# Moving the chunk states' products behind the outputs' products, and splitting one product in two, in a fused SSD and PReLU kernel

## Chip, cores and metric

One core of a Trainium2 chip runs the whole kernel. The metric is device time in microseconds of one execution; the time before is the median of six runs, 374.7 us (374.41 to 375.7). Engines: TensorE (PE; its weight loads appear as PEld), VectorE (DVE), ScalarE (ACT), GpSimd (POOL), and SyncE (SP), whose queue issues nearly all DMAs.

## What is computed

First a Mamba-2 style scan (batch 4, 8 heads, 768 tokens, head size 32, state size 16), then an MLP with a leaky activation over its 3072 tokens:

```python
for c in range(nc):                                   # chunks in order
    cum = np.cumsum(log_a[:, :, sl], axis=-1)
    L = np.exp(cum[:, :, :, None] - cum[:, :, None, :]) * causal
    CB = np.einsum('bhin,bhjn->bhij', Cc, Bc)
    y_intra = np.einsum('bhij,bhjd->bhid', CB * L, xc)
    y_inter = np.einsum('bhin,bhnd->bhid', Cc, state) * np.exp(cum)[:, :, :, None]
    y[:, :, sl] = y_intra + y_inter
    Bx = np.einsum('bhjn,bhjd->bhjnd', Bc, xc) * decay_from_j[:, :, :, None, None]
    state = decay_full[:, :, None, None] * state + np.sum(Bx, axis=2)
# x: y as 3072 tokens of 256
h = x @ w_in                                          # 256 -> 2048
g = np.maximum(h, 0.0) + alpha * np.minimum(h, 0.0)
out = g @ w_out                                       # 2048 -> 256
```

All data are fp32, and each fp32 product shows as two passes ("x2") in the trace.

## The kernel before

**Work and stages.** The tokens fall into 24 chunks of 128, taken in 12 pairs; two pairs make a group of 512 tokens, and there are six groups. Pair p yields the scan's outputs of its tokens, group g puts them through the MLP. In group 0 the MLP is done plainly, mixed with the conversion of the weights and with pairs 0 to 3. In groups 1 to 5 both MLP products are done as 2x2 block products with seven multiplications in place of eight (a Winograd form). While group g goes through the MLP, the two pairs of group g + 1 are computed in between.

**A quad.** A group's MLP has four quads z = 0 to 3, each for four blocks of 128 of the hidden size (`quad`, L758). A quad makes seven hidden products, each of two matmuls of 128x256 (L770), in two PSUM banks A and Y: b11 into A, t1 into Y, t2 onto A, t3 onto A, b22 onto Y, then t4 onto A. Y is emptied in between (g12 is made of it by `prelu`: ScalarE L753, then VectorE L755), and ScalarE writes m1 back into it (L799) so that b21 can be added onto it. After b21 comes the last `prelu`, which makes g11 of Y. The differences of g11, g12, g21, g22 are made on GpSimd (L804, L813). They are the inputs of the seven products with `w_out` (`product`, L734), which run one quad later.

**The order is written out by hand.** Each engine works its queue in the order of the program. `quad` calls `after(j)` at fourteen slots j, and `after` (L1024) puts everything else there: `places` says in which slot which of the seven products of the quad in front goes, `steps` in which slot a pair takes its next stage, `ahead` in which the GpSimd product `bn` (B times decays, L385) of a coming pair is made. b21 stands between slots 10 and 11.

**A pair's stages** (`pair`, L416; a generator, `ssm` takes steps of it). Pairs 4 to 11 are called fine. A fine pair has nine stages before the change:

1. transposes of B and C (L469), a copy (L472)
2. to 5. four quarters of the decay scans on VectorE (`half_decays`, L438), with the last ScalarE's `spread_c`
6. `states(added(...))`: `added` (L514) makes the state products (L519), column tiles of 128x64, in a PSUM tile of its own; `states` (L524) reads them on VectorE (ScalarE where the batch starts), and masks the result on GpSimd (`sm`). Then GpSimd's `c_decayed` (`cd`)
7. `products_bc` (L562): the Gram products (L569), row tiles of 32x128, four of them side by side, r = 0 to 3: r = 0 and 1 in small banks ("ss"), r = 2 and 3 in the hidden banks ("hp", those that A and Y have); and VectorE's first two multiplications by them (L604)
8. the other two multiplications
9. the outputs y: products with the state (L620, tiles of 64x128) and with the decayed Gram (L627, 128x32) in two ss banks, and two ScalarE copies into `xts` (L634)

The last pair of each batch (5, 8, 11) needs the state products of one chunk, not two: eight passes at L519 become four.

For the pair `nxt` = 2g + 2, stages 3 to 5 stand in slots 1, 2, 5 of quad 0, stage 6 in slot 9, stage 7 in slot 13, stages 8 and 9 in slots 1 and 5 of quad 1. The pair after it has stages 1 and 2 in slots 12 and 14 of quad 1 and the rest in quads 2 and 3 likewise. Quads 0 and 2 are called even here, 1 and 3 odd. In even quads with a pair (`with_gram`) product 7 stands in slot 11, behind b21; elsewhere (`without`) in slot 9, ahead of it. The first quad of group 1 has no products of a quad in front; rest of group 0's outputs (L684) take their places (`last_out`).

**PSUM.** ss and hp tiles rotate over two banks each; `bank(i)` are four fixed banks for the seven products' sums (and for group 0's outputs, which `store_first`, L688, copies out).

Of the kernel before, what the change touches and what calls it, by code (L numbers as in the profile page):

```python
# [9 lines left out]
F32 = mybir.dt.float32  # L10
# [12 lines left out]
def kernel(  # L23
# [25 lines left out]
    nc = tc.nc  # L49
# [276 lines left out]
    held = {}  # L326
    bns = {}

    def identity_bank():


        m5_bank.append(bank(3))
        nc.scalar.copy(out=m5_bank[0][:, HT:], in_=ident_h[:, :HT])
        ident_p.append(m5_bank[0][:, HT:])
# [77 lines left out]
    def spare():  # L412

        return ps_h.tile([P, GT], F32, name="hp", tag="hp")

    def pair(gp):  # L416

        b, c = divmod(2 * gp, CPB)
        nat, abc, xt, ap = loads["p", gp]
        last = c + 2 == CPB  # L420
        dec = work.tile([P, 2, H, Q], F32, name="dec")
        dv = dec.rearrange("p k h t -> p k (h t)")

# [37 lines left out]
            yield  # L461


        tp = spare() if gp == 1 else ss_tile()
        if gp == 0:
            keep_warm(tp, 3, Q)
# [19 lines left out]
        def c_decayed():  # L486
            nc.gpsimd.tensor_tensor(out=cd.rearrange("p k t -> p (k t)"), in0=ct, in1=pf,
                                    op=ALU.mult)

        fine = gp >= 2 * GC // 2  # L490
        if gp < 2:
            spread_c()
        if gp == 0:
# [1 line left out]
            dps = spare()  # L495
            keep_warm(dps, 6, Q)
            yield
        bn = bns.pop(gp) if gp in bns else pair_loads(gp)
        if gp == 1:
            c_decayed()  # L500
            dps = spare()
# [1 line left out]
        elif gp:  # L503
            yield

        nk = 1 if last else 2
        st = [masked.get(b)]  # L510
        new = work.tile([P, 2, P], F32, name="state")
        sm = work.tile([P, 2, P], F32, name="sm")

        def added(dps):  # L514
            dps = dps.rearrange("p (k m) -> p k m", m=P)
            for k in range(nk):
                for w in range(KC):
                    ws = slice(64 * w, 64 * w + 64)
                    nc.tensor.matmul(dps[ws, k], bn[:, k, ws], xt[:, k, w * P : (w + 1) * P],  # L519
                                     start=True, stop=True, tile_position=(0, 64 * w),  # L520
                                     skip_group_check=True)
            return dps

        def states(dps):  # L524
            for k in range(nk):
                old = state.get(b)
                if old is None:
                    nc.scalar.copy(out=new[:, k], in_=dps[:, k])
                else:
                    e = (k + 1) * Q - 1  # L530
                    nc.vector.scalar_tensor_tensor(out=new[:, k], in0=old, scalar=pf[:, e : e + 1],
                                                   in1=dps[:, k], op0=ALU.mult, op1=ALU.add)
                state[b] = new[:, k]
            nc.gpsimd.tensor_tensor(out=sm[:, :nk], in0=new[:, :nk],
                                    in1=hmask.unsqueeze(1).to_broadcast([P, nk, P]), op=ALU.mult)
            st.extend(sm[:, k] for k in range(nk))
            masked[b] = st[-1]

        if fine:
            for k in range(2):  # L540
                for w in range(2):
                    half_decays(k, w)
                    if k == 1 and w == 1:
                        spread_c()
                    yield
        else:
            if gp > 1:
                states(added(ss_tile()))
                c_decayed()
            decays(0)  # L550
            if gp == 1:
                dps = added(dps)
            if gp:
                yield
            if gp != 1:
                decays(1)
            if gp > 1:
                spread_c()
# [24 lines left out]
        if gp == 0:  # L583
            gram = products_bc()
            dps = added(dps)
            yield
            c_decayed()
            times(dec[:, :, :2], one_less(gram))
        elif gp == 1:
            decays(1)  # L590
            gram = products_bc()
            g0 = one_less(gram)
            states(dps)
            times(dec[:, :, :2], g0)
        else:
            if fine:
                states(added(ss_tile()))
                c_decayed()
            yield
            gram = products_bc()  # L600
        for i, r in enumerate(r for r in ((2, 3, 0, 1) if fine else (3, 2, 1, 0) if gp > 1 else range(4))
                              if r in gram):
# [6 lines left out]
        yield  # L609


        y = [ss_tile()[:, : 2 * Q].rearrange("p (k t) -> p k t", k=2) for w in range(KC)]
        if gp < 2:
            keep_warm(y[0].rearrange("p k t -> p (k t)"), 2 - gp)
        begun = False
# [7 lines left out]
        for k in range(2):  # L623
            for w in range(KC):
                for q in range(4):
                    h = 4 * w + q
                    nc.tensor.matmul(y[w][32 * q : 32 * q + 32, k], xt[:, k, h * D : (h + 1) * D],  # L627
                                     dec[:, k, h], start=False, stop=True,
                                     tile_position=(0, 32 * q), skip_group_check=True)
        g, q = divmod(2 * gp, GC)  # L630
        if q == 0:
            xts[g] = xtp.tile([P, KC, GT], F32, name="xT")
# [98 lines left out]
    LAST = {**HALVES, 4: (3, 1)}  # L731
    blocks = {}

    def product(g, z, n):  # L734

        if z == 0 and n == 1:
            ms[g] = [t.rearrange("p (h t) -> p h t", h=2)
                     for t in [bank(i) for i in range(3)] + m5_bank]
        i, h = (LAST if g == NG - 1 else HALVES)[n]
        s1, s2, s4 = out_sums  # L740
        for p in range(2):
            q = 2 * z + p
            w = {1: wq[:, q, 0, 0], 2: wq[:, q, 1, 0], 3: s4[:, q], 4: wq[:, q, 1, 1],
                 5: s1[:, q], 6: s2[:, q], 7: wq[:, q, 0, 1]}[n]
            nc.tensor.matmul(ms[g][i][:, h], w, blocks[g, z][n][:, p],  # L745
                             start=(q == 0 and h == 0), stop=(q == NQ - 1),
                             skip_group_check=True)
# [227 lines left out]
    for f in range(FIRST, NF):  # L975
        if f in (5, 10):
            load_pair(3 + f // 10)
        if f == 5:
            load_rows(1)
        hidden(0, f)  # L980
        if f <= 10:
            ssm(2)
        if f >= 9:
            ssm(3)
        if f < FIRST + 2:
            convert_a(*pieces[f + 1 + (f > FIRST)])
        convert_next(first=f > FIRST)
        if f == FIRST:
            convert_a(*pieces[6])
        if f == 8:  # L990
            bns[3] = pair_loads(3)
        if f == 8:
            rows_clamp(1)
            held["pr"] = rows_scan(1)
            rows_out(1)
        output(f - FIRST)
        if f in in_steps:
            weight_sums(wi, in_sums, 0, in_steps[f])
    early[0] = None
    token_sums(1)  # L1000
    ssm(2 * GC // 2, 2)


    steps = {(0, 1): 0, (0, 2): 0, (0, 5): 0, (0, 9): 0, (0, 13): 0, (1, 1): 0, (1, 5): 0,
             (1, 12): 1, (1, 14): 1, (2, 1): 1, (2, 2): 1, (2, 5): 1, (2, 9): 1, (2, 13): 1,
             (3, 1): 1, (3, 5): 1, (3, 12): 2, (3, 14): 2}

    late_sums = {(0, 2): ((wqt, out_sums, 0, 0),), (0, 4): ((wqt, out_sums, 0, 1),),
# [6 lines left out]
    last_out = {3: ((0, 0),), 5: ((1, 0),), 7: ((2, 0),), 8: ((3, 0),), 11: ((0, 1),), 13: ((1, 1),),  # L1015
            14: ((2, 1), (3, 1))}

    with_gram = {3: 1, 5: 2, 7: 3, 8: 5, 11: 7, 13: 6, 14: 4}
    without = {3: 1, 5: 2, 7: 3, 8: 5, 9: 7, 13: 6, 14: 4}
    for i in range(NZ * (NG - 1)):  # L1020
        g, z = divmod(NZ + i, NZ)
        nxt = 2 * g + 2

        def after(j, g=g, z=z, i=i, nxt=nxt):  # L1024
            places = with_gram if nxt < NP and z % 2 == 0 else without
            if i and j in places:
                product(*divmod(NZ + i - 1, NZ), places[j])
            if i == 0:
                for f, half in last_out.get(j, ()):
                    output(NF - LATE + f, half)  # L1030
            if (i, j) in ((0, 13), (1, 8)):
                store_first(i)
            for args in late_sums.get((i, j), ()):
                weight_sums(*args)
            if g > 1 and z == 0 and j in (5, 9, 13, 14):
                if j == 5:
                    comb[0] = combine(g - 1)
                next(comb[0], None)
            if g > 1 and z in (1, 3) and j == 11:
                finish(g - 1, z // 2)  # L1040
            if nxt + steps.get((z, j), NP) < NP:
                ssm(nxt + steps[z, j])
            if nxt < NP and (z, j) == (3, 7):
                token_sums(g + 1)
            ahead = nxt + {(1, 3): 1, (3, 8): 2}.get((z, j), NP)
            if ahead < NP:
                if ahead == 6:
                    rows_turn(1, held["pr"])
                bns[ahead] = pair_loads(ahead)

        comb = [None] if i == 0 else comb
        if z == 0 and nxt < NP:
            load_pair(nxt + 1)
        if z == 2 and nxt + 2 < NP:
            load_pair(nxt + 2)
        quad(g, z, after)
# [31 lines left out]
```

## Time and profile before

| | |
|---|---|
| median of six runs | 374.7 us (374.41 to 375.7) |
| the profiled execution | 374.95 us; span from first to last instruction 373.2 us; granted TensorE clock 1.000 |
| PE idle in waits that the profile lists | under 5 us, the largest 1.7 us for bn at L519 and 1.2 us for the first operand |
| 560 passes of the seven products (L745) | 82.5 us (with `w_out`) and 58.3 us (with its sums) busy |
| 64 passes of the state products in ss banks (L519) | 5.7 us busy |
| DMA | 30.71 MB in all, HBM read 26.98 MB |

A line of the timeline has start (us from the span's start), duration, engine, line, operation, tiles written and read, shape and count, and in brackets the engine's idle time ahead of it with what ended it. Several instructions of one kind in a row are one line. Matmuls are pipelined, so that durations of PE overlap: the time that a run costs is the difference of two starts.

### The profile page before, as it was taken

To read this page: it belongs to the slowest core of one execution; us is meant where nothing else is said; L and a number is where in the kernel's file an instruction comes from. 1 tells how busy PE (TensorE), PEld (TensorE's weight loads), DVE (VectorE), ACT (ScalarE), POOL (GpSimd) and SP (SyncE) were. 2 spreads that over 40 slices of the span, in tenths; PEclk is the share of its full clock that TensorE was granted. 3 is DMA by queue.
4 is the path that set the end of the run, shared out by engine and by line. 5 is a ranking of instruction groups with operands and counts; after the bars stand their busy time and mean duration, and the time that the engine had idled before them with its cause. 6 is when DMAs were issued, how large, how long until landed. Compare 5 with 4: busy or idle time off the path is not lost.

```text
span 373.2 us, 6183 instructions
## 1 busy us (share of the span) xinstructions
PE 365.1 (98%) x2223; PEld 294.1 (79%) x2223; DVE 243.3 (65%) x462; ACT 179.3 (48%) x384; POOL 200.9 (54%) x211
## 2 busy tenths in 40 slices
PE   8899999999999999999999999999999999999996
PEld 7676666578778788788788788788788788888884
DVE  7897889976438647838638847637847644543364
ACT  1557856435255345444445445445535525553541
POOL 4875566777928744724645535455355355264512
PEclk9999999999999999999999999999999999999999
DMA  7989998911019501003703702801911001001003
GB/s 139 195 173 338 240 302 163 173 47 58 28 48 186 105 3 56 2 0 58 154 3 57 155 2 51 163 0 30 157 28 29 2 0 22 10 0 30 1 0 84
DMA packets 121878, 30.71 MB, mean 82 GB/s; under 512 B 93736, under 2 KB 117752, under 8 KB 121848
## 3 DMA queue, kind: packets, MB, share of 16 engines
q1 hardware_dynamic: 116736, 29.74, 36.6%
q10 hardware_dynamic: 5112, 0.59, 1.1%
q8 instruction: 17, 0.28, 0.3%
q14 instruction: 13, 0.11, 0.1%
HBM read 26.98 MB, written 3.34 MB: 81 GB/s over the span
## 4 chain that ended last, share of the span: by engine, by line
PE 87%; DMA 3%; DVE 3%; POOL 2%; ACT 1%; ACTq 1%; issue 1%; POOLq 0%; DVEq 0%
PE hp L770 33%; PE bank L745 32%; PE bank L684 6%; PE hp L646 4%; PE ss L627 2%; DMA raw<-in_moe_w_in_dram 2%; PE ss L569 2%; PE ss L620 1%; DVE dec L438 1%; PE ss L519 1%; PE hp L569 1%; PE hp L661 1%; PE ss L469 1%; DMA nat<-in_C_dram 1%; ACTq L163 1%
## 5 line engine op out<-in xcount | busy, mean ns | idle before, releaser
L813 POOL TENSOR_TENSOR gt<-gt 128x512 f32<-128x512 f32 x58 | 73.6, 1269 | 31.4 <-DVE gt L755 24.5
L755 DVE SCALAR_TENSOR_TENSOR gt<-hp,s_mul,gt 128x256 f32<-128x256 f32 x120 | 52.5, 479 | 47.6 <-ACT gt L753 46.3
L745 PE MATMUL bank<-gt,w_out 128*128 128x256 f32 x320 | 82.5, 382 | 0.4 <-ACT o_sb L691 0.4
L753 ACT ACTIVATE gt<-hp,s_alpha 128x256 f32<-128x256 f32 x120 | 50.3, 470 | 46.8 <-PE hp L770 32.7
L745 PEld LDWEIGHTS bank<-gt,w_out 128*128 128x128 f32 x320 | 60.0, 190 | 11.2 <-issue 2.3
L804 POOL TENSOR_TENSOR gt<-gt 128x512 f32<-128x512 f32 x20 | 25.4, 1271 | 79.1 <-DVE gt L755 79.1
L745 PE MATMUL bank<-gt,ws 128*128 128x256 f32 x240 | 58.3, 379 | 0.0
L745 PEld LDWEIGHTS bank<-gt,ws 128*128 128x128 f32 x240 | 45.1, 190 | 5.8
L438 DVE TENSOR_TENSOR_SCAN dec<-abc,bank 128x256 f32<-128x256 f32 x80 | 48.1, 661 | 0.0
L770 PE MATMUL hp<-xs,w_in 128*128 128x256 f32 x160 | 42.9, 390 | 0.0
L770 PE MATMUL hp<-xT,w_in 128*128 128x256 f32 x160 | 41.9, 384 | 0.0
L770 PE MATMUL hp<-xs,ws 128*128 128x256 f32 x160 | 41.1, 379 | 0.0
L789 DVE TENSOR_TENSOR hp<-hp,u 128x512 f32<-128x512 f32 x20 | 14.0, 699 | 39.8 <-ACT u L787 39.8
L778 ACT COPY m<-hp 128x512 f32<-128x512 f32 x20 | 11.7, 586 | 51.8 <-PE hp L770 51.8
L770 PEld LDWEIGHTS hp<-xs,w_in 128*128 128x128 f32 x160 | 28.7, 189 | 7.7 <-issue 3.0
L770 PEld LDWEIGHTS hp<-xT,w_in 128*128 128x128 f32 x160 | 29.7, 190 | 5.1 <-issue 1.2
L770 PEld LDWEIGHTS hp<-xs,ws 128*128 128x128 f32 x160 | 30.4, 190 | 4.1
L684 PE MATMUL bank<-w_out,gt 128*128 128x256 f32 x128 | 31.0, 384 | 0.0
L684 PEld LDWEIGHTS bank<-w_out,gt 128*128 128x128 f32 x128 | 23.7, 190 | 6.6 <-issue 3.5
L793 DVE TENSOR_TENSOR c<-hp,m 128x512 f32<-128x512 f32 x20 | 13.6, 682 | 19.3 <-PE hp L770 19.3
L646 PE MATMUL hp<-xT,w_in 128*128 128x512 f32 x48 | 22.8, 597 | 0.8 <-DVE gt L650 0.6
L787 ACT COPY u<-hp 128x512 f32<-128x512 f32 x20 | 11.7, 585 | 23.0 <-PE hp L770 23.0
(156 smaller groups left out, 552.9 us busy)
## 6 DMA issues: line engine op xcount, KB each, us to landing
abc<-z SPq DMA_DIRECT2D x20, 512.0 KB, 5.2
raw<-in_moe_w_in_dram SPq DMA_DIRECT2D x8, 512.0 KB, 5.3
raw<-in_moe_w_out_dram SPq DMA_DIRECT2D x8, 512.0 KB, 6.8
xt<-in_x_dram SPq DMA_DIRECT2D x24, 128.0 KB, 2.9
out_dram<-o_sb SPq DMA_DIRECT2D x32, 64.0 KB, 1.9
nat<-in_B_dram SPq DMA_DIRECT2D x22, 64.0 KB, 2.7
nat<-in_C_dram SPq DMA_DIRECT2D x22, 64.0 KB, 2.8
ap<-pf SPq DMA_DIRECT2D x11, 128.0 KB
```

Source lines behind the costliest of these rows:

```text
L438: nc.vector.tensor_tensor_scan(out=dv[:, k, hs], data0=abc[k][:, hs], data1=ident_p[0], initial=0.0, op0=ALU.mult, op1=ALU.add)
L646: nc.tensor.matmul(hp, w_in[:, k, f * P : (f + 1) * P], xts[g][:, k], start=(k == 0), stop=(k == KC - 1))
L684: nc.tensor.matmul(pos[0][t // 2][:, t % 2], gt[:, t * Q : (t + 1) * Q], w_out[:, f], start=(f == 0 and t % 2 == 0), stop=(f == NF - 1), s ...
L745: nc.tensor.matmul(ms[g][i][:, h], w, blocks[g, z][n][:, p], start=(q == 0 and h == 0), stop=(q == NQ - 1), skip_group_check=True)
L753: nc.scalar.mul(o[:, p], h[:, p], s_alpha[:, fs[p]])
L755: nc.vector.scalar_tensor_tensor(out=o[:, p], in0=h[:, p], scalar=s_mul[:, fs[p]], in1=o[:, p], op0=ALU.mult, op1=ALU.max)
L770: nc.tensor.matmul(to[:, p], w(2 * z + p), b, start=start and p == 0, stop=True, skip_group_check=True)
L778: nc.scalar.copy(out=m1, in_=A)
L789: nc.vector.tensor_tensor(out=Y, in0=Y, in1=u2, op=ALU.add)
L793: nc.vector.tensor_tensor(out=c22, in0=A, in1=m5, op=ALU.add)
L804: nc.gpsimd.tensor_tensor(out=tc_, in0=g22, in1=g12, op=ALU.subtract)
L813: eng.tensor_tensor(out=o, in0=x0, in1=x1, op=ALU.subtract)
```

## The change

- A fine pair takes eleven stages. `added` and `states` come first and in stages of their own, before the transposes; `c_decayed` moves to the last quarter of the decay scans; y's products and their copies become two stages.
- In slot 5 of the odd quads four stages follow each other: y's products of the pair in front, the state products of the next pair, the copies of y, the states of the next pair. The state products are written into the free second half of y's second PSUM tile (`beside`), so they need no tile of their own. Pair 4, which has no fine pair in front, takes its first four stages ahead of the first quad.
- Slot 9 of the even quads loses its stage. In even quads with a pair one half of product 7 goes into slot 9 (ahead of b21), the other stays in slot 11.
- `bn` of the coming pair is made in slot 9 of the even quads rather than in slots 3 and 8 of quads 1 and 3 (pair 4's during block 14 of group 0).
- `store_first(1)` moves from slot 8 to slot 2 of the second quad of group 1.

```diff
         if fine:
+            bn = bns.pop(gp) if gp in bns else pair_loads(gp)
+            dps = added(beside.pop(gp) if gp in beside else ss_tile()[:, : 2 * Q])
+            yield
+            states(dps)
+            yield
...
         if fine:
             for k in range(2):
                 for w in range(2):
                     half_decays(k, w)
                     if k == 1 and w == 1:
                         spread_c()
+                        c_decayed()
                     yield
...
         else:
-            if fine:
-                states(added(ss_tile()))
-                c_decayed()
-            yield
+            if not fine:
+                yield
             gram = products_bc()
...
-        y = [ss_tile()[:, : 2 * Q].rearrange("p (k t) -> p k t", k=2) for w in range(KC)]
+        ys = [ss_tile() for w in range(KC)]
+        y = [t[:, : 2 * Q].rearrange("p (k t) -> p k t", k=2) for t in ys]
+        if fine:
+            beside[gp + 1] = ys[1][:, 2 * Q :]
...
+        if fine:
+            yield
         g, q = divmod(2 * gp, GC)
...
-    def product(g, z, n):
+    def product(g, z, n, parts=(0, 1)):
...
-        for p in range(2):
+        for p in parts:
...
+        if f == 14:
+            bns[4] = pair_loads(4)
...
-    ssm(2 * GC // 2, 2)
+    ssm(2 * GC // 2, 4)
-    steps = {(0, 1): 0, (0, 2): 0, (0, 5): 0, (0, 9): 0, (0, 13): 0, (1, 1): 0, (1, 5): 0,
-             (1, 12): 1, (1, 14): 1, (2, 1): 1, (2, 2): 1, (2, 5): 1, (2, 9): 1, (2, 13): 1,
+    steps = {(0, 1): 0, (0, 2): 0, (0, 5): 0, (0, 13): 0, (1, 1): 0, (1, 5): 0,
+             (1, 12): 1, (1, 14): 1, (2, 1): 1, (2, 2): 1, (2, 5): 1, (2, 13): 1,
              (3, 1): 1, (3, 5): 1, (3, 12): 2, (3, 14): 2}
...
-    with_gram = {3: 1, 5: 2, 7: 3, 8: 5, 11: 7, 13: 6, 14: 4}
-    without = {3: 1, 5: 2, 7: 3, 8: 5, 9: 7, 13: 6, 14: 4}
+    both = (0, 1)
+    without = {j: (n, both) for j, n in {3: 1, 5: 2, 7: 3, 8: 5, 9: 7, 13: 6, 14: 4}.items()}
+    with_gram = {**without, 9: (7, (0,)), 11: (7, (1,))}
...
-            if (i, j) in ((0, 13), (1, 8)):
+            if (i, j) in ((0, 13), (1, 2)):
                 store_first(i)
...
                 ssm(nxt + steps[z, j])
+                if j == 5 and z % 2:
+                    for p in (1, 0, 1):
+                        if nxt + z // 2 + p < NP:
+                            ssm(nxt + z // 2 + p)
...
-            ahead = nxt + {(1, 3): 1, (3, 8): 2}.get((z, j), NP)
+            ahead = nxt + {(0, 9): 1, (2, 9): 2}.get((z, j), NP)
```

More of the change, by code (lines that the diff above doesn't have):

```diff
@@ L327 @@
     bns = {}
+    beside = {}
     def identity_bank():
@@ L420, in pair @@
         last = c + 2 == CPB
+        fine = gp >= 2 * GC // 2
         dec = work.tile([P, 2, H, Q], F32, name="dec")
@@ L461, in pair, with added, states @@
             yield
+        nk = 1 if last else 2
+        st = [masked.get(b)]
+        new = work.tile([P, 2, P], F32, name="state")
+        sm = work.tile([P, 2, P], F32, name="sm")
+        def added(dps):
+            dps = dps[:, : 2 * Q].rearrange("p (k m) -> p k m", m=P)
+            for k in range(nk):
+                for w in range(KC):
+                    ws = slice(64 * w, 64 * w + 64)
+                    nc.tensor.matmul(dps[ws, k], bn[:, k, ws], xt[:, k, w * P : (w + 1) * P],
+                                     start=True, stop=True, tile_position=(0, 64 * w),
+                                     skip_group_check=True)
+            return dps
+        def states(dps):
+            for k in range(nk):
+                old = state.get(b)
+                if old is None:
+                    nc.scalar.copy(out=new[:, k], in_=dps[:, k])
+                else:
+                    e = (k + 1) * Q - 1
+                    nc.vector.scalar_tensor_tensor(out=new[:, k], in0=old, scalar=pf[:, e : e + 1],
+                                                   in1=dps[:, k], op0=ALU.mult, op1=ALU.add)
+                state[b] = new[:, k]
+            nc.gpsimd.tensor_tensor(out=sm[:, :nk], in0=new[:, :nk],
+                                    in1=hmask.unsqueeze(1).to_broadcast([P, nk, P]), op=ALU.mult)
+            st.extend(sm[:, k] for k in range(nk))
+            masked[b] = st[-1]
+        if fine:
[4 more added lines that the diff above has]
+            yield
         tp = spare() if gp == 1 else ss_tile()
@@ L488, in c_decayed @@
                                     op=ALU.mult)
-        fine = gp >= 2 * GC // 2
         if gp < 2:
@@ L497, in pair @@
             yield
-        bn = bns.pop(gp) if gp in bns else pair_loads(gp)
+        if not fine:
+            bn = bns.pop(gp) if gp in bns else pair_loads(gp)
         if gp == 1:
@@ L504, in pair @@
             yield
[L509 to L537, printed above, removed]
         if fine:
@@ L595, in pair @@
         else:
-            if fine:
-                states(added(ss_tile()))
-                c_decayed()
-            yield
+            if not fine:
+                yield
             gram = products_bc()
@@ L629, in pair @@
                                      tile_position=(0, 32 * q), skip_group_check=True)
+        if fine:
+            yield
         g, q = divmod(2 * gp, GC)
@@ L1026, in after @@
             if i and j in places:
-                product(*divmod(NZ + i - 1, NZ), places[j])
+                product(*divmod(NZ + i - 1, NZ), *places[j])
             if i == 0:
```

## The prediction

> **What bounds the kernel now.** I read the busy shares and the chain of waits first, then TensorE's timeline around the places that the change touches.
>
> ```profile
> PE 365.1 (98%) x2223; PEld 294.1 (79%) x2223; DVE 243.3 (65%) x462; ACT 179.3 (48%) x384; POOL 200.9 (54%) x211
> ...
> PE 87%; DMA 3%; DVE 3%; POOL 2%; ACT 1%; ACTq 1%; issue 1%; POOLq 0%; DVEq 0%
> ```
>
> TensorE (PE) sets the end: from 82 us on it starts a pass of a 128x256 product every 0.216 us (four passes, one product of two steps, take 0.86 us from start to start). The number of products doesn't change. So only what lies between them counts: changes of the array's tiling, and waits. The wait list of PE holds under 5 us in all, but a wait inside a run of small products isn't in it. The timeline of an even quad (pair 6) shows the part that is rearranged; the columns are start, duration (the last end is modelled, so I use differences of starts), engine, line.
>
> ```profile
> 149.71 1.03 PE L770 MATMUL hp<-xs,w_in 128*128 128x256 f32 x4
> 150.67 0.66 PE L519 MATMUL ss<-xt,bn 128*64 128x128 f32 x8
> 151.25 1.13 PE L770 MATMUL hp<-xT,w_in 128*128 128x256 f32 x4
> 152.22 1.03 PE L745 MATMUL bank<-gt,w_out 128*128 128x256 f32 x4
> 153.09 1.03 PE L745 MATMUL bank<-gt,ws 128*128 128x256 f32 x4
> 154.04 0.48 PE L569 MATMUL ss<-cz,bc 32*128 32x256 f32 x2
> ...
> 155.34 1.13 PE L745 MATMUL bank<-gt,w_out 128*128 128x256 f32 x4
> ```
>
> In order: the t4 product, the state products, the b21 product, product 7, product 6, the Gram products, product 4. Zooming into the Gram run, its fourth row tile (r = 3, in a hidden-product bank "hp") starts late, and the engines beside it tell why:
>
> ```profile
> 154.29 0.48 PE L569 MATMUL hp<-cz,bc 32*128 32x256 f32 x1
> ```
> ```profile
> 152.48 0.84 ACT L753 ACTIVATE gt<-hp,s_alpha 128x256 f32<-128x256 f32 x2 [0.38 <-PE hp L770]
> ```
> ```profile
> 153.35 0.88 DVE L755 SCALAR_TENSOR_TENSOR gt<-hp,s_mul,gt 128x256 f32<-128x256 f32 x2 [0.45 <-ACT gt L753]
> ```
> ```profile
> 95.04 0.18 PEld L569 LDWEIGHTS hp<-cz,bc 32*128 32x128 f32 x1 [0.26 <-DVE gt L755]
> ```
>
> That bank is Y, which b21 has just filled. It is free only when ScalarE and VectorE have made g11 of it: 153.35 + 0.88 = 154.23, and r = 3 starts 0.06 later. Tile 0 stood ready at 154.04, so 0.24 us is lost. In the first quad of group 1 the same wait (last line) is 0.55 us, as other VectorE work stands ahead. This release sits a fixed 154.29 - 151.25 = 3.04 us behind b21's start; nothing else is in its way, since both engines idle for it (0.38 and 0.45 us).
>
> **What the Trainium skill says.** The Trainium skill, page "TensorEngine Tiling (Array Packing)", Tiling Modes, Key Properties: a change of tiling mode, not of tile alone, drains TensorE. The trace agrees: the state products come 0.10 us after t4's last slot, and the first b21 pass takes 0.32 instead of 0.216 us. The Trainium skill, "TensorE: Matmul & The Clock Gate", Step-by-step: what each phase is for: MATMULs stay in program order. At 95.04 to 95.06 the chunk's second half of the Gram products starts only once r = 3 has, so one late tile holds all behind it. The Trainium skill, "PSUM — Partial Sum Buffer", PSUM bank collisions raise a hardware error: two engines may not touch one bank and quadrant at once, even in other columns. No run here shows it; it matters because the state products now share a bank with y.
>
> **The change, part by part.**
>
> 1. State products leave slot 9 of the even quads (pairs 5 to 11; pair 4 apart). From t4's start to product 4's start such a quad now takes 155.34 - 149.71 = 5.63 us with eight passes (pairs 6, 7, 9, 10), 5.41 with four (120.93 to 126.34; the last pair of a batch: 5, 11), 5.50 for pair 8, whose VectorE instruction was late. New course from t4: 0.86, half of product 7 0.43, so b21 starts at 1.30. It needs the copy of m1 into Y (L799), which ends at 0.90 to 1.00 (1.36 in pair 8's quad): no wait. Then b21 0.86, other half 0.43, product 6 0.86, entry 0.09: the Gram products arrive at 3.55. r = 3 needs b21's start + 3.04 less the 0.10 of the drain that is gone: 1.30 + 2.93 = 4.23. The wait grows from 0.24 to 0.68. From r = 3 to product 4 takes 155.34 - 154.29 = 1.05: product 4 at 5.28. Gain: 0.35 for pairs 6, 7, 9, 10; 0.13 for 5 and 11; 0.22 for 8. So half the price of the removed products comes back as a longer wait.
>
> 2. They are added behind the y products (L620, L627) of the pair in front:
>
> ```profile
> 160.72 0.49 PE L620 MATMUL ss<-cd,sm 64*128 64x128 f32 x4
> 161.14 1.08 PE L627 MATMUL ss<-dec,xt 128*32 128x128 f32 x32
> 162.15 1.13 PE L770 MATMUL hp<-xs,w_in 128*128 128x256 f32 x4
> 163.12 0.38 PE L770 MATMUL hp<-xT,ws 128*128 128x256 f32 x1
> ```
>
> The run leaves the full array and comes back anyway (0.97 instead of 0.86 for L770). Added: four steps of 0.109 us (two column tiles side by side; two steps for the last pair of a batch) and one inner change of mode. No row shows 128x32 to 128x64; the nearest, L620 to L627, costs 0.09, and I take 0.11. It can't gain, as the passes are extra; at most it is the price alone in slot 9, 0.34. So 0.55 and 0.33 us (up to 0.78 and 0.56). Net of 1 and 2: 4 x 0.20 + 2 x 0.20 + 0.11 = 1.3 us slower.
>
> 3. Copies and state steps: ScalarE's two copies (0.65 us) may wait for the 0.2 to 0.5 us of state products, and VectorE's two steps (0.34 to 0.72) go ahead of c22. Even one behind the other they end about 1.6 us after the products, and c22 0.7 later; ScalarE wants c22 only after g12, 3.1 us after. Hidden by t3 and b22; without that cover, up to 0.7 us in seven quads. GpSimd's sm, cd and bn steps (0.72, 0.72, 0.64) move into slots where it idles 5 us, or behind L804; nat of pairs 8 to 11 has landed by then (pair 9's last issue at 205.2, some 2.7 us to land, wanted after 208.8). Zero.
>
> 4. Pair 4: its state products now go ahead of the first quad, isolated as before: +0.78 at 81.72. GpSimd makes bn at about 80.4, 0.64 long, so at about 81.0: no wait (bound: 0.5 if the weight sums go first). token_sums is 0.64 later; its first result, at 82.95, is wanted after 83.8. In slot 9 nothing stands between t4 and b21: b21 starts at 1.05 instead of 1.54: L799's end at 0.90 plus 0.15, which t3 takes to start behind u2's copy in pair 6's quad (146.04 to 146.18). The weight sum on VectorE (0.69) then sets g11; r = 3 at 4.43 instead of 4.89: gain 0.47. Net +0.31.
>
> 5. store_first(1) moves from slot 8 to slot 2 of the second quad:
>
> ```profile
> 107.55 1.03 PE L770 MATMUL hp<-xs,w_in 128*128 128x256 f32 x4
> 109.02 1.13 PE L745 MATMUL bank<-gt,w_out 128*128 128x256 f32 x4 [0.44 <-ACT o_sb L691]
> 109.99 1.03 PE L770 MATMUL hp<-xT,w_in 128*128 128x256 f32 x4
> ```
>
> 107.55 to 109.99 is 2.44 where two products are 1.73: gain 0.71. The copy (0.58) fits into ScalarE's 1.20 us of idling ahead of u2. The DMA queue is held by this store until 108.99 and gets free sooner for pair 6's loads; nobody waits for those. rows_turn (about 0.12 us of PE) only changes place.
>
> Sum: 1.3 + 0.31 - 0.71 = +0.9 us. The profiled execution took 374.95 (span 373.2 and 1.75 around it), so 375.85; that run lies 0.25 above the median of 374.7, so the median becomes **375.6**.
>
> **Rivals.**
> - **The Gram wait doesn't grow (faster).** Y's release keeps its distance to the Gram products: product 4 at 3.55 + 0.24 + 1.05 = 4.84, a gain of 0.79 or 0.57 against 0.55 or 0.33 added, so -0.24 in seven quads; with 4 and 5, -2.1: 372.6. This is what the split of product 7 would give if only b21's own wait counted. Deciding point: r = 3 freed 0.13 us earlier than I say balances the change. Against: the chain PE, ACT, DVE has no slack in any of the quads looked at. 15%.
> - **The y block pays full price (slower).** The switch to 128x64 costs as an isolated one: 0.23 more in seven quads, 377.2. For: the mode does change. Against: L620 to L627. 12%.
> - **Hardly a change.** The inner switch is free (-0.1 x 7), the early insertion half hidden: 374.8. 18%.
> - My case, 375.6, with 375.1 to 376.2 as its own bounds: 55%. That the change doesn't do what it says can't be: the order of TensorE's queue is written out.
>
> **How the numbers follow.** About 0.2% (0.75 us) is what a measurement of this kernel can tell from no change, and my case straddles that line: seven tenths of it lie above 375.45. Slower: 0.55 x 0.7 + 0.12 = 0.50. Faster: 0.15 and a little of the third rival, 0.19. Same: 0.31. The range leaves out the faster rival and half of the dear one: 374.2 to 377.0.
>
> **What would show it.** Right: in even quads b21 starts 1.30 after t4, and r = 3 of the Gram products about 0.7 us after the other three tiles; y and state products together take 0.55 or 0.33 more than y did; no wait for o_sb. Wrong: r = 3 less than 0.5 late, or the run behind y over 0.7 longer, or a wait of b21 for L799, or late c22 in odd quads.

## The result, and the profile after

The changed kernel takes 375.94 us (median of 15 runs, 375.59 to 377.22); the kernel before, in the same session, 374.52 us (34 runs). The ratio is 1.0035, 95% interval 1.0025 to 1.0046: slower, by about 1.3 us. Forecast were 375.6 us and +0.9. The profiled execution took 376.65 us with a span of 374.7 (before: 374.95 and 373.2).

```profile
PE 367.1 (98%) x2223; PEld 295.5 (79%) x2223; DVE 247.1 (66%) x462; ACT 180.3 (48%) x384; POOL 201.2 (54%) x211
...
PE 89%; DVE 4%; DMA 2%; POOL 2%; ACT 1%; issue 1%; POOLq 0%; DVEq 0%; ACTq 0%
```

The page says little: the same 2223 passes on a TensorE that looks just as busy. The timeline of the same even quad (pair 6; lines have moved, L519 is now L478, L745 L758, L770 L783, L569 L579) shows what happened. Columns as before: start, duration, engine, line.

```profile
150.45 1.03 PE L783 MATMUL hp<-xs,w_in 128*128 128x256 f32 x4
151.31 0.59 PE L758 MATMUL bank<-gt,w_out 128*128 128x256 f32 x2
151.74 1.03 PE L783 MATMUL hp<-xT,w_in 128*128 128x256 f32 x4
152.61 0.59 PE L758 MATMUL bank<-gt,w_out 128*128 128x256 f32 x2
153.04 1.03 PE L758 MATMUL bank<-gt,ws 128*128 128x256 f32 x4
153.99 0.48 PE L579 MATMUL ss<-cz,bc 32*128 32x256 f32 x2
...
155.73 1.13 PE L758 MATMUL bank<-gt,w_out 128*128 128x256 f32 x4
```

t4, half of product 7, b21, the other half, product 6, Gram products, product 4. From t4 to product 4 it is now 155.73 - 150.45 = 5.28 us, where it was 5.63. The eight passes that left cost 0.78 us by themselves; the other 0.43 went into the wait of r = 3, the fourth row tile of the Gram products. Here are its first pass and the VectorE instruction that frees its bank:

```profile
154.67 0.48 PE L579 MATMUL hp<-cz,bc 32*128 32x256 f32 x1
154.68 0.48 PE L579 MATMUL ss<-cz,bc 32*128 32x256 f32 x2
```
```profile
153.74 0.88 DVE L768 SCALAR_TENSOR_TENSOR gt<-hp,s_mul,gt 128x256 f32<-128x256 f32 x2 [0.35 <-ACT gt L766]
```

g11 is done at 154.62, r = 3 starts at 154.67, 0.66 us behind its turn (before: 0.24); the other tiles' second half stands in the queue behind it (154.68). The odd quad holds the products that moved:

```profile
161.10 0.49 PE L631 MATMUL ss<-cd,sm 64*128 64x128 f32 x4
161.53 1.08 PE L638 MATMUL ss<-dec,xt 128*32 128x128 f32 x32
162.54 0.66 PE L478 MATMUL ss<-xt,bn 128*64 128x128 f32 x8
163.12 1.13 PE L783 MATMUL hp<-xs,w_in 128*128 128x256 f32 x4
```

162.54 to 163.12 is what is new: 0.59 us, unrounded. So a pair with two chunks' states wins 0.35 us in the even quad and pays 0.59 in the odd one.

**Where the time went.** The last run of group 0's outputs starts at times that differ by up to 1.6 us from one execution to the next (79.1 to 80.7 us in thirteen of the fourteen traces of this study, 79.7 and 80.1 in the two of the changed kernel itself; the fourteenth, with the state products issued twice, comes to 81.8), so spans of single executions can't be compared. The stretches from there on are the same to 0.01 us in the two traces of the changed kernel, and where other kernels have the same quad, to 0.04. From b11 to b11 of successive quads, after less before:

| stretch | forecast | measured |
|---|---|---|
| ahead of the first quad: pair 4's states | +0.78 | +0.74 |
| first quad | -0.47 | -0.27 |
| second quad: y with pair 5's states; store_first(1) | +0.33 - 0.71 | +0.37 - 0.71 |
| even quads of pairs 6, 7, 9, 10 | 4 x -0.35 | 4 x -0.35 |
| even quads of pairs 5, 8, 11 | -0.13, -0.22, -0.13 | -0.02, -0.22, -0.14 |
| odd quads, two chunks' states (four) | 4 x +0.55 | 4 x +0.59 |
| odd quads, one chunk's (8, 11) | 2 x +0.33 | 2 x +0.37 |
| rows_turn out of an odd quad | (counted even) | -0.12 |
| sum | +0.9 | +1.3 |

`rows_turn` is one small transpose (L370, 96x96) that goes with `bn` of pair 6, and so moved from an odd quad into pair 5's even quad. It had cost about 0.12 us where it was: -0.02 and -0.12 together are the -0.13 forecast. In its new place it stands ahead of b21 (122.50, b21 at 122.59). The sum of the stretches is the measured difference.

### The profile page after: what moved, and what is told of

The parts are those of the page before. It is cut to its first block, busy times and chain, and to the rows that moved or that the text cites. A ratio compares the mean times of both kernels' runs of the same rounds, so it can differ in the third digit from the quotient of the medians.

```text
span 374.7 us, 6170 instructions
## 1 busy us (share of the span) xinstructions
PE 367.1 (98%) x2223; PEld 295.5 (79%) x2223; DVE 247.1 (66%) x462; ACT 180.3 (48%) x384; POOL 201.2 (54%) x211
## 4 chain that ended last, share of the span: by engine, by line
PE 89%; DVE 4%; DMA 2%; POOL 2%; ACT 1%; issue 1%; POOLq 0%; DVEq 0%; ACTq 0%
PE hp L783 33%; PE bank L758 32%; PE bank L697 5%; PE hp L659 4%; PE ss L638 2%; DMA raw<-in_moe_w_in_dram 2%; PE hp L579 2%; PE ss L631 1%; PE ss L579 1%; DVE dec L441 1%; PE ss L478 1%; PE hp L674 1%; PE ss L511 1%; PE hp L270 1%; DVE gt L663 1%
## 5 line engine op out<-in xcount | busy, mean ns | idle before, releaser
L758 PE MATMUL bank<-gt,w_out 128*128 128x256 f32 x320 | 83.5, 381 | 0.0
L758 PEld LDWEIGHTS bank<-gt,w_out 128*128 128x128 f32 x320 | 60.1, 190 | 10.4 <-issue 2.3
L758 PE MATMUL bank<-gt,ws 128*128 128x256 f32 x240 | 58.3, 379 | 0.0
L758 PEld LDWEIGHTS bank<-gt,ws 128*128 128x128 f32 x240 | 45.1, 190 | 5.8
L783 PE MATMUL hp<-xs,w_in 128*128 128x256 f32 x160 | 42.8, 390 | 0.0
L783 PE MATMUL hp<-xT,w_in 128*128 128x256 f32 x160 | 41.2, 380 | 0.0
L783 PE MATMUL hp<-xs,ws 128*128 128x256 f32 x160 | 41.1, 379 | 0.0
L783 PEld LDWEIGHTS hp<-xs,w_in 128*128 128x128 f32 x160 | 28.7, 189 | 7.5 <-issue 2.3
L783 PEld LDWEIGHTS hp<-xs,ws 128*128 128x128 f32 x160 | 30.4, 190 | 4.1
L783 PEld LDWEIGHTS hp<-xT,w_in 128*128 128x128 f32 x160 | 30.2, 190 | 4.4 <-ACT hp L812 0.3
L493 POOL TENSOR_TENSOR sm<-state,bmask 128x256 f32<-128x256 f32 (+1 forms) x12 | 7.6, 637 | 35.0 <-DVE state L490 35.0
```

Source lines behind the costliest of these rows:

```text
L758: nc.tensor.matmul(ms[g][i][:, h], w, blocks[g, z][n][:, p], start=(q == 0 and h == 0), stop=(q == NQ - 1), skip_group_check=True)
L783: nc.tensor.matmul(to[:, p], w(2 * z + p), b, start=start and p == 0, stop=True, skip_group_check=True)
```

## Experiments

Each kernel was timed beside runs of the kernel before, whose medians were 374.53 to 374.85 us. The theory, called chain theory below: product 4 of an even quad comes at b21's start + 2.93 (b21, ScalarE, VectorE, then r = 3) + 1.05 us, as long as r = 3 has to wait. Passes ahead of b21 then count in full, and passes between b21 and the Gram products are free until the wait is filled. The main rival: TensorE's own sum of passes and mode changes, with order of no account.

**Product 7 whole behind b21.**

```diff
-    with_gram = {**without, 9: (7, (0,)), 11: (7, (1,))}
+    with_gram = {j: p for j, p in without.items() if j != 9}
+    with_gram[11] = (7, both)
```

> The changed kernel with product 7 whole in slot 11, behind b21, and nothing in slot 9. Chain theory (product 4 of an even quad stands a fixed 2.93 + 1.05 us behind b21's start, whatever lies between): b21 waits for the copy of m1 and starts at about 1.06 after t4 in place of 1.30, product 4 comes at 5.1 to 5.2 in place of 5.28, so 0.7 to 1.2 us less over seven quads: about 375.0. Rival, TensorE's own sum (order doesn't matter, the loss is only the state products' price in the y block): b21's new wait of 0.2 to 0.3 us is lost and nothing comes back, 1.5 to 2 us more: 377.5.

Measured: 374.7 us, ratio to before 1.0002 (0.9992 to 1.0012): 1.2 less than the changed kernel. Pair 6's quad:

```profile
149.02 1.03 PE L783 MATMUL hp<-xs,w_in 128*128 128x256 f32 x4
150.09 1.13 PE L783 MATMUL hp<-xT,w_in 128*128 128x256 f32 x4
151.05 1.03 PE L758 MATMUL bank<-gt,w_out 128*128 128x256 f32 x4
...
153.12 0.48 PE L579 MATMUL hp<-cz,bc 32*128 32x256 f32 x1
...
154.18 0.48 PE L758 MATMUL bank<-gt,w_out 128*128 128x256 f32 x1
```

b21 does wait (0.20 us after t4's last slot), and its first pass then takes 0.32 us instead of 0.216, as after a change of tiling; so r = 3 (153.12) comes 3.03 us behind its start and not 2.93. Yet product 4 comes at 5.16 in place of 5.28, and the seven even quads together are 1.28 us shorter than in the changed kernel: against the kernel before nothing is left of the loss (0.03 us by the stretches). A TensorE that idles and starts b21 sooner is faster here than one that does useful passes first.

**Product 7 whole ahead of b21** (`with_gram = without`).

> The changed kernel with product 7 whole in slot 9, ahead of b21. Chain theory: b21 starts 0.43 us later (1.73 after t4), and product 4 with it (5.71), though TensorE does the same work: 7 x 0.43 = 3.0 us more, 378.9, and r = 3 of the Gram products waits 1.1 us. Rival, TensorE's own sum: no difference, 375.9.

Measured: 379.09 us, ratio 1.0122 (1.0103 to 1.014), 3.15 more than the changed kernel.

```profile
150.43 1.03 PE L783 MATMUL hp<-xs,w_in 128*128 128x256 f32 x4
151.29 1.03 PE L758 MATMUL bank<-gt,w_out 128*128 128x256 f32 x4
152.15 1.03 PE L783 MATMUL hp<-xT,w_in 128*128 128x256 f32 x4
...
155.08 0.48 PE L579 MATMUL hp<-cz,bc 32*128 32x256 f32 x1 [0.40 <-DVE gt L768]
...
156.14 0.48 PE L758 MATMUL bank<-gt,w_out 128*128 128x256 f32 x1
```

b21 at 1.73, r = 3 another 2.93 later, product 4 at 5.71: 0.43 us more in each of the seven quads for the same work. The rival of a mere sum is out.

**The split alone, in the kernel before** (states stay in slot 9; `product` takes `parts`, `with_gram` as in the change).

> The kernel before with product 7 alone split into halves around b21; the state products stay in slot 9 as well. Chain theory: b21 starts 0.43 us later in the seven even quads with a pair, and product 4 with it, though TensorE does the same work: 7 x 0.43 = 3.0 us more, 377.6. Rival, TensorE's own sum: 374.6.

Measured: 377.16 us, ratio 1.0063 (1.0045 to 1.008). Stretch by stretch: +0.43 in six even quads, +0.34 in pair 8's, nothing elsewhere, 2.9 in all (2.6 by the medians). The split alone is a loss; in the change it takes the place of the state products as what delays b21.

**The store alone, in the kernel before.**

```diff
-            if (i, j) in ((0, 13), (1, 8)):
+            if (i, j) in ((0, 13), (1, 2)):
```

> The kernel before with store_first(1) alone moved from slot 8 to slot 2. My account: the wait of product 7 for the o_sb copy (0.44 us and what lies around it) goes and nothing is late in its place, 0.71 us less, 373.9. Rival: ScalarE's copy delays u2 in its new slot and the gain is given back, 374.6.

Measured: 373.84 us, ratio 0.9981 (0.9972 to 0.999). The only stretch that differs is the second quad, by 0.71. This part of the change is good by itself.

**State products issued twice behind y.**

```diff
-            dps = added(beside.pop(gp) if gp in beside else ss_tile()[:, : 2 * Q])
+            again = gp in beside
+            room = beside.pop(gp) if gp in beside else ss_tile()[:, : 2 * Q]
+            for i in range(2 if again else 1):
+                dps = added(room)
```

> The changed kernel with the state products behind y issued twice (the second writes the same values). Both theories: only passes are added, no change of mode, 0.44 us for two chunks and 0.22 for one, 4 x 0.44 + 3 x 0.22 = 2.4 us more, 378.3; the run is then split into 0.44 of passes and 0.15 of mode change. Rival (the shared PSUM bank makes copies and states late and the cover in the odd quad is thin): more than 0.44 more, with c22 or b21 of the odd quads late.

Measured: 379.46 us (four runs, 378.53 to 380.68), ratio 1.0132 (1.0107 to 1.0156), about a microsecond more than forecast. The stretches from the first quad on give 2.4 more than the changed kernel's, as forecast; the profiled execution (380.68) lost the rest in its first 80 us, where its granted clock was 0.91 over the first 20 us. The other three, at a clock of 1.000, lie at 378.53 to 379.98; what they have above 378.3 stays open, and the reading rests on the stretches.

```profile
164.81 1.09 PE L478 MATMUL ss<-xt,bn 128*64 128x128 f32 x16
165.83 0.92 PE L786 MATMUL hp<-xs,w_in 128*128 128x256 f32 x3
```

164.81 to 165.83 is 1.02 us where it was 0.59: the odd quads' runs grew by 0.44 (two chunks) and 0.22. So of the 0.59 and 0.37 paid behind y the passes are 0.44 and 0.22 and the inner mode change 0.15. The odd quads grew by no more than that, so c22 and b21 there weren't late.

**bn later** (`ahead` back to odd quads, slot 3 of both).

> The changed kernel with bn made in slot 3 of the odd quads, no longer in slot 9 of the even ones. If GpSimd's bn slowed the weight sum that VectorE makes at that moment in the first quad (1.05 us in place of 0.69), that sum is back at 0.69, r = 3 of the Gram products there is 0.36 earlier, and the time 0.3 to 0.4 less, 375.6. Rival: the 1.05 has another cause, nothing changes in the first quad, 375.9.

Measured: 376.1 us, ratio 1.0036 (1.0022 to 1.0049): the median can't tell 0.3. The trace can. VectorE and GpSimd in the first quad, first in the changed kernel:

```profile
93.77 1.05 DVE L726 TENSOR_TENSOR w_out<-w_out 128x512 f32<-128x512 f32 x1
94.74 0.86 DVE L768 SCALAR_TENSOR_TENSOR gt<-hp,s_mul,gt 128x256 f32<-128x256 f32 x2
```
```profile
93.63 0.64 POOL L387 TENSOR_TENSOR bn<-nat,prt 128x256 f32<-128x256 f32 x1
```

and with bn elsewhere:

```profile
93.65 0.68 DVE L726 TENSOR_TENSOR w_out<-w_out 128x512 f32<-128x512 f32 x1
94.25 0.87 DVE L768 SCALAR_TENSOR_TENSOR gt<-hp,s_mul,gt 128x256 f32<-128x256 f32 x2
```

The weight sum (L726) takes 0.68 instead of 1.05 us, and the first quad wins 0.64 over before in place of 0.27: the 0.37 was bn's. `rows_turn` went back with bn, and pair 5's even quad shows -0.13 and the odd quad behind it its full +0.59.

**Pair 4's states back in slot 9 of the first quad** (timed on two occasions, the second time beside the changed kernel).

```diff
-    ssm(2 * GC // 2, 4)
+    ssm(2 * GC // 2, 2)
...
+            if (i, j) == (0, 9):
+                ssm(nxt)
```

> The changed kernel with pair 4's state products back in slot 9 of the first quad of group 1 (the states of pairs 5 to 11 stay behind y). My account from the two traces: 0.74 us ahead of the first quad goes, 0.27 us in the first quad comes back, 0.5 us less, 375.45. Rival: the early insertion was hidden by the waits of the start, then 0.27 more, 376.2.

> The changed kernel with pair 4's states back in slot 9 once more, as its median (376.41, six runs) and its trace (0.4 us less than the changed kernel from one stage to the next) disagree. By the trace 375.5, by the first median 376.4.

> The changed kernel once more, beside the next one on the same chip: 375.9 as measured.

Measured: 376.41 us (six runs, ratio 1.0042, 1.0026 to 1.0057), then 375.74 (eleven, 1.0027, 1.001 to 1.0043) with the changed kernel beside it at 376.06 (ten, 1.0035, 1.0021 to 1.0049). The stretches say 0.74 less ahead of the first quad, 0.32 more in it and no change behind it. The intervals overlap: a gain of 0.4 fits, but the medians don't show it.

**Transposes as cover, on top of the change.** The next pair's transposes move from slot 12 of the odd quad to slot 11 of the even one, ahead of the states' stages (the tiles of the states and of `cz` are then taken later).

```diff
-             (1, 12): 1, (1, 14): 1, ...
-             (3, 1): 1, (3, 5): 1, (3, 12): 2, (3, 14): 2}
+             (0, 11): 1, (1, 14): 1, ...
+             (3, 1): 1, (3, 5): 1, (2, 11): 2, (3, 14): 2}
```

> The changed kernel with the next pair's four transposes (0.44 us) in slot 11 of the even quad, between b21 and the Gram products, in place of slot 12 of the odd quad; the state products stay behind y. Chain theory: there they fill the wait of r = 3 (0.66 down to about 0.23 us) and cost nothing, and the odd quad gets 0.44 shorter: 7 x 0.44 = 3.1 us less, 372.8, less than both kernels. Rival, TensorE's own sum: they cost the same anywhere, 375.9. Risk: ScalarE's copy of the transposes stands behind g11 there, and the second small Gram bank waits for it.

Measured: 372.99 us, ratio 0.9959 (0.9946 to 0.9972).

```profile
149.13 1.03 PE L789 MATMUL hp<-xs,w_in 128*128 128x256 f32 x4
...
151.72 0.60 PE L510 MATMUL ss<-ident,nat 128*128 128x128 f32 x4
152.16 1.03 PE L764 MATMUL bank<-gt,ws 128*128 128x256 f32 x4
...
154.41 1.13 PE L764 MATMUL bank<-gt,w_out 128*128 128x256 f32 x4
```

Four transposes more between b21 and the Gram products, and product 4 still comes at 5.28: 0.44 us of TensorE work for nothing, seven times. With pair 4's states back as well:

> The changed kernel with the transposes in slot 11 and pair 4's state products back in slot 9 of the first quad. If the early insertion costs what its local times say (0.74 less 0.3): 372.99 - 0.4 = 372.6. Rival, hidden in the start: 373.3.

Measured: 372.41 us, ratio 0.994 (0.9919 to 0.996), 0.6 less than without (0.43 by the stretches).

**Transposes as cover and the store, without the state move.** The same move in the kernel before, with store_first(1) in slot 2.

> The kernel before, states still in slot 9, with store_first(1) in slot 2 and the next pair's transposes in slot 11 of the even quad. Chain theory: the transposes (0.44 us) fill r = 3's wait of 0.24, so the even quad gets 0.20 longer and the odd one 0.44 shorter: 7 x 0.24 = 1.7 us, and 0.71 from the store: 372.1. That would be a little under the same change on top of the state move, since two chunks' states cost 0.59 behind y and only 0.55 more in slot 9. Rival, the state move is what makes room for the transposes: then this gains nothing but the store, 373.8.

Measured: **371.84 us**, ratio 0.9927 (0.9907 to 0.9947), the fastest here and below both kernels. The stretches give 2.5 us less than before (0.71 for the store; 0.44 less in seven odd quads, 0.22 more in six even ones); the medians are 3.0 apart, with an interval from 2.0 to 3.5.

```profile
147.65 1.03 PE L774 MATMUL hp<-xs,w_in 128*128 128x256 f32 x4
148.60 0.66 PE L522 MATMUL ss<-xt,bn 128*64 128x128 f32 x8
149.19 1.13 PE L774 MATMUL hp<-xT,w_in 128*128 128x256 f32 x4
150.16 1.03 PE L749 MATMUL bank<-gt,w_out 128*128 128x256 f32 x4
151.02 0.60 PE L469 MATMUL ss<-ident,nat 128*128 128x128 f32 x4
151.46 1.03 PE L749 MATMUL bank<-gt,ws 128*128 128x256 f32 x4
152.42 0.48 PE L573 MATMUL ss<-cz,bc 32*128 32x256 f32 x2
...
153.49 1.13 PE L749 MATMUL bank<-gt,w_out 128*128 128x256 f32 x4
```

The Gram run takes 1.07 us from its start to product 4, where it took 1.30 before and 1.74 after the change: r = 3 no longer waits. The state products ahead of b21 fill the wait for m1, and the transposes behind it fill the wait of r = 3. Moving the states was not what made room.

## Why the prediction held, step by step

- **Step 1, even quads: right.** b21 at 1.30, r = 3 at 4.22 (4.23 forecast), product 4 at 5.28 (5.28). The two product 7 experiments moved b21 by -0.23 and +0.43 and product 4 by -0.12 and +0.43 (the first is 0.10 short for b21's slow first pass after the wait), so it is b21's start that counts, not how many passes stand behind it. The rival in which the wait doesn't grow is refuted, and with it the only case that was faster.
- **Step 2, behind y: right in kind, short in one term.** The inner mode change was taken at 0.11 from the nearest row; it is 0.15 (0.59 less 0.44). The row was read short: its 0.09 is the gap ahead of the first step at L627, and that step takes 0.134 us too, where the others take 0.109, so the change there costs about 0.12. Over seven pairs the term is short by 0.3 of the missing 0.4 us. The rival of a full second price (0.34 of fixed cost) is refuted: less than half of that is paid. The rival of hardly a change falls on the same 0.15, which isn't free, and on the 0.74 of the early insertion, which isn't half hidden. The Trainium skill, "TensorEngine Tiling (Array Packing)", Key Properties, says that a change of tiling mode drains TensorE; the trace agrees: the first of the state products comes 0.11 us late at this change too (162.54, where y's last step, at 162.31 and 0.109 long, ends at 162.42).
- **Step 3, copies and states: the waiting was there, and hidden.** ScalarE's second copy now waits for the state products, and VectorE's steps for that copy:

```profile
163.24 0.37 ACT L647 COPY xT<-ss 128x256 f32<-128x256 f32 x1 [0.41 <-PE ss L478]
```
```profile
163.65 0.73 DVE L490 SCALAR_TENSOR_TENSOR state<-state,ap,ss 128x128 f32<-128x128 f32 x2 [1.98 <-ACT xT L647]
164.29 0.69 DVE L806 TENSOR_TENSOR c<-hp,m 128x512 f32<-128x512 f32 x1
```

  The two touch different columns of one bank, and the program lets one after the other at it, as the PSUM page named in the prediction asks; a collision itself no run here shows. VectorE's sum c22 (L806) is still in time: the odd quads lengthen by the 0.59 and 0.37 of the state products' run alone.
- **"Zero" for GpSimd's moved steps was wrong in one place.** bn in slot 9 of the first quad meets the weight sum that VectorE makes there of two parts of w_out, and delays g11 by 0.37. The Trainium skill, "SBUF — State Buffer", Who interferes with whom, says that a VectorE instruction with two SBUF inputs contends with a GpSimd instruction that reads SBUF; the trace agrees, with 1.05 against 0.68 us. I had asked only whether GpSimd was free. The kernel before had such a meeting at the same place, with GpSimd's `sm`:

```profile
93.51 0.69 DVE L713 TENSOR_TENSOR w_out<-w_out 128x512 f32<-128x512 f32 x1
```
```profile
93.74 1.04 POOL L534 TENSOR_TENSOR sm<-state,bmask 128x256 f32<-128x256 f32 x1 [1.24 <-DVE state L531]
```

  There the sum started first and kept its 0.69 us, and sm took 1.04 in place of 0.73 (GpSimd's spans are rough here), off the path. After the change bn starts first (93.63, the sum at 93.77), and the sum pays.
- **Step 4: +0.47 in place of +0.31**, and nearer than its terms were, as they partly cancel: 0.37 more for bn; 0.10 less because b21 started at 0.95 and not at 1.05 (0.05 us behind the copy of m1, not the 0.15 of t3 behind u2); 0.08 less because r = 3, with bn elsewhere, comes 3.30 behind b21 and not 3.38 (4.43 less 1.05); 0.04 less for the insertion. Only the stretches show it, as the medians of the two pair 4 runs differ by more.
- **Step 5: right,** 0.71 in the change and alone. Product 7 no longer waits for o_sb in the second quad:

```profile
108.54 1.03 PE L783 MATMUL hp<-xs,w_in 128*128 128x256 f32 x4
109.40 1.03 PE L758 MATMUL bank<-gt,w_out 128*128 128x256 f32 x4
110.27 1.03 PE L783 MATMUL hp<-xT,w_in 128*128 128x256 f32 x4
```

## What to carry to other kernels

Where TensorE waits for the end of a chain through other engines, taking its work out from between the chain's start and end gains nothing, as the wait grows by as much. Find the instruction that starts the chain (here b21), start it as early as can be, and put passes that are due anyway between it and the chain's end. The state products' run cost a fixed 0.34 us alone and 0.15 behind another run of small products, so moving it saved 0.19; but it moved out of a quad in which half of its 0.78 came back as a longer wait. When a step is moved to a "free" slot of GpSimd, look at what VectorE reads at that moment.

## What was not expected of the hardware

A change of tiling between two runs of small products costs 0.15 us from 128x32 to 128x64, and about 0.12 from 64x128 to 128x32, much of it a gap and the rest a longer first step (0.160 and 0.134 us instead of 0.109).

And a wait cost TensorE more than its own length: the first pass of b21 after 0.20 us of waiting (product 7 behind b21) takes 0.32 us instead of 0.216, as much as the first full-array pass after small ones. The whole b21 takes 0.97 us there, product 7 after the wait for o_sb in the kernel before 0.97, and an undisturbed product 0.86. Where t3 comes 0.07 us late behind u2's copy (146.18 in the kernel before), its first pass takes 0.29. So the waits looked at here cost 0.07 to 0.10 us on top; why, no run shows.
